# Attention and a routed mixture of experts on one core: splitting two of expert 0's weight chunks, wider products from expert 1 on, and a sum shared between ScalarE and VectorE

## The chip, the cores and the metric

The kernel runs on one NeuronCore of a Trainium2 chip. The metric is the device time of one execution in microseconds. Five engines with queues of their own work side by side: TensorE (PE, with its weight loads as PEld), VectorE (DVE), ScalarE (ACT), GpSimd (POOL) and SyncE (SP), which here only issues DMAs. TensorE writes its results to PSUM, of which the expert stage uses eight banks; all else lives in SBUF.

## What is computed

Causal attention over 4 batches of 12 heads, 448 rows of 64, feeds 1792 tokens of width 768 into a mixture of 8 experts. Tokens go to experts greedily by score, at most 224 to each; each expert applies two layers with a ReLU between.

```python
scores = np.where(mask, -1e9, scale * q @ k.T);  attn = softmax(scores)
x = (attn @ v).transpose(0, 2, 1, 3).reshape(1792, 768)
order = np.argsort(-(x @ w_gate).flatten())        # greedy, 224 tokens for each expert
for e in range(8):
    out[assigned == e] = np.maximum(x[assigned == e] @ w1[e], 0) @ w2[e]
```

## The kernel before

The program is written out by a planner. Each step is a task with an engine, an estimated duration, a priority and the tasks that it depends on; `Schedule.run` (line 117) gives each engine's next instruction to the ready task of highest priority, and fills TensorE's idle time with dummy products (`filler`, line 1130) until expert 0 starts. The order in each queue is thus fixed when the program is built, by estimated durations, and a queue that meets a wait holds everything behind it.

**Attention** runs over 24 pairs of heads: scores (line 218), masked exponential (228, 238), transposes of the probabilities (246), product with v (272), copy to `xt`. A pair's rows are then transposed back (`rows_at` and `rows_mm`, line 296), scaled by the reciprocal of the row sums into `xio` (320) and stored batch by batch to the DRAM buffer `xd` (325). Pairs from `LATE` = 10 on are not transposed there but in `late` (line 941), beside the routing of expert 0: four transposes of a pair into one PSUM bank of four that rotate, then each half of the bank (two of four blocks) scaled by ScalarE with four instructions (314) or by VectorE with two (320), whichever the planner finds free. `PIECES` says after which pairs a piece of a batch is stored.

**Routing** finds each expert's 224 tokens in turn by counting on TensorE (`rt`, lines 767, 784) and comparing on VectorE (666, 781, 750). `members` (813) turns the choice into indices: a one-hot `oh` of 128 positions (841) times token numbers (849), cast to `idx` (852). The steps of experts 0 and 1 have priority 10.9; from expert 2 on (`calm`, line 911) a VectorE step has 5.0 and a TensorE step is planned 0.4 us later. A gather by GpSimd (1121) brings an expert's rows from `xd`; for expert 0 it waits for all stores.

**Experts.** An expert's weights are eight chunks of 768 KB, four of the first layer and four of the second, fetched by SP (1100) into four raw buffers. Each chunk is split into `wh`, a rounded copy that ScalarE casts (1106), and `wl`, the remainder, three differences by VectorE (1112). Only the first four chunks of expert 0 (g < 4) are used whole. The inputs are split likewise (1160, 1165). A first-layer block f of 128 outputs is a sum over six d:

- expert 0: one float32 product of 224 columns each (1177), or two of 112 for f < 2;
- expert 1: three products of 224 columns (1184, 1185, 1186);
- from expert 2 on (`TWICE` = 2): one product of `wh` with both input parts side by side, 448 columns (1182), and one of `wl` with 224 (1186). The two halves of the bank are then added by a VectorE reduce (`mid_sum`, 1196).

ReLU and its split (1192, 1200) follow, then the second layer: three products for each of eight f, two halves of the rows and two of the columns (1212), eviction by ScalarE (1216) and scatter by GpSimd (1231). The tiles `ph`, three banks, take the first-layer sums in turn; the four `po` banks take the second layer's.

## Time and profile before

| | us |
|---|---|
| median of 3 runs | 503.19 (502.56 to 503.5) |
| the profiled execution | 503.2 |
| its span, first to last instruction | 501.5 |
| TensorE busy | 488.0 |
| VectorE busy | 394.5 |
| ScalarE busy | 292.9 |

The span is what the trace shows; 1.7 us of the execution's time lie outside it. A busy share is an average over stages with different limits, so the stages are read one by one. In a row of the timeline, the number in brackets is how long the engine sat idle before the instruction and what ended that.

### The profile page before, as it was taken

The numbers are of one execution on the slowest core, as the hardware profiler recorded it, in microseconds if no ns is written. First come the engines' busy times: TensorE is split into PE (matmuls) and PEld (weight loads), VectorE is DVE, ScalarE is ACT, GpSimd is POOL, SyncE is SP. The second block draws the span as 40 slices with busy tenths as digits, with TensorE's granted clock in tenths as the row PEclk, the third lists the DMA queues.
The fourth block names the chain that finished last, engine by engine and source line by source line (L and its number), as shares of the span: only waits on it lengthen the run. The fifth ranks groups of instructions, "written<-read, shape, count | busy, mean of one in ns | idle before, by whom it ended". The sixth has DMA issues, their size and how long they took to land.

```text
span 501.5 us, 10644 instructions
## 1 busy us (share of the span) xinstructions
PE 488.0 (97%) x3930; PEld 406.5 (81%) x3930; DVE 394.5 (79%) x1308; ACT 292.9 (58%) x741; POOL 51.8 (10%) x86
## 2 busy tenths in 40 slices
PE   8999999999999979999999999999999999999995
PEld 4666666666666665998999999999999999999995
DVE  4978777787789685688999999999999788687710
ACT  5988888989888571244545624444453545654410
POOL 5000000000000101010120120120211410110101
PEclk9999999999999999999999999999999999999999
DMA  8932182542000048766967663584672976858101
GB/s 230 302 109 99 38 269 63 184 148 75 2 2 1 1 121 253 257 195 191 320 217 247 220 213 127 160 289 139 219 234 79 349 242 225 286 181 308 57 1 55
DMA packets 19349, 84.08 MB, mean 168 GB/s; under 512 B 2272, under 2 KB 5280, under 8 KB 19296
## 3 DMA queue, kind: packets, MB, share of 16 engines
q1 hardware_dynamic: 16624, 72.36, 44.8%
q0 software_dynamic: 2672, 11.04, 7.1%
q8 instruction: 31, 0.51, 0.4%
q14 instruction: 22, 0.18, 0.1%
HBM read 72.38 MB, written 11.01 MB: 166 GB/s over the span
## 4 chain that ended last, share of the span: by engine, by line
PE 88%; DMA 4%; ACT 2%; POOL 2%; issue 1%; DVE 1%; POOLq 0%; DVEq 0%; ACTq 0%; SPq 0%
PE po L1212 26%; PE ph L1182 13%; PE t L246 10%; PE s L272 10%; PE ph L1186 7%; PE s L218 7%; PE t L218 2%; DMA xio<-xd,idx 2%; PE rt L767 2%; PE ph L1147 2%; PE t L296 1%; PE t L331 1%; PE po L1177 1%; PE ph L1184 1%; PE ph L1185 1%
## 5 line engine op out<-in xcount | busy, mean ns | idle before, releaser
L1112 DVE TENSOR_TENSOR wl<-wr,wh 128x512 fp32r<-128x512 f32 x180 | 115.9, 682 | 9.0 <-ACT wh L1106 9.0
L1106 ACT CAST wh<-wr 128x1536 fp32r<-128x1536 f32 x60 | 88.4, 1479 | 59.1 <-DMA wr<-in_w 58.9
L238 ACT ACTIVATE P<-Sm,mx 112x224 f32<-112x224 f32 (+2 forms) x192 | 99.1, 523 | 22.5 <-DVE mx L228 17.2
L1182 PE MATMUL ph<-xhl,wh 128*128 128x448 f32 x288 | 94.0, 380 | 0.0
L1186 PE MATMUL ph<-xhl,wl 128*128 128x224 f32 x336 | 89.7, 267 | 0.0
L1212 PE MATMUL po<-wh,HH 128*112 128x384 f32 x256 | 68.3, 343 | 0.0
L1212 PE MATMUL po<-wl,HH 128*112 128x384 f32 x256 | 68.0, 341 | 0.0
L1212 PE MATMUL po<-wh,HL 128*112 128x384 f32 x256 | 67.2, 338 | 0.0
L228 DVE CUSTOM_DVE_ANT_0 Sm<-s,MK 112x448 f32<-112x448 f32 (+1 forms) x144 | 59.6, 464 | 6.3 <-PE s L218 5.6
L1186 PEld LDWEIGHTS ph<-xhl,wl 128*128 128x128 f32 x336 | 64.2, 191 | 0.0
L1182 PEld LDWEIGHTS ph<-xhl,wh 128*128 128x128 f32 x288 | 54.2, 188 | 4.2
L246 PE MATMUL t<-idf,P 112*112 112x112 f32 x480 | 52.6, 262 | 0.4 <-ACT P L238 0.4
L272 PE MATMUL s<-PT,v 112*64 112x448 f32 (+3 forms) x384 | 50.6, 405 | 0.0
L246 PEld LDWEIGHTS t<-idf,P 112*112 112x112 f32 x480 | 45.8, 133 | 5.1 <-ACT P L238 1.5
L1192 ACT ACTIVATE HH<-hs 128x224 fp32r<-128x224 f32 x48 | 18.8, 391 | 49.0 <-DVE hs L1196 47.5
L1212 PEld LDWEIGHTS po<-wh,HL 128*112 128x112 f32 x256 | 43.9, 174 | 0.3
L1212 PEld LDWEIGHTS po<-wl,HH 128*112 128x112 f32 x256 | 43.3, 175 | 0.4
L252 ACT COPY PT<-t 112x448 f32<-112x448 f32 (+1 forms) x109 | 42.7, 465 | 1.2 <-PE t L246 1.1
L1212 PEld LDWEIGHTS po<-wh,HH 128*112 128x112 f32 x256 | 43.2, 175 | 0.2
L218 PE MATMUL s<-raw 64*112 64x112 f32 (+2 forms) x288 | 41.3, 414 | 0.1
L1196 DVE TENSOR_REDUCE hs<-ph 128x224 f32<-128x448 f32 x48 | 29.9, 622 | 14.3 <-PE ph L1186 10.0
L272 PEld LDWEIGHTS s<-PT,v 112*64 112x64 f32 x384 | 23.2, 136 | 21.3 <-issue 9.8
(169 smaller groups left out, 667.5 us busy)
## 6 DMA issues: line engine op xcount, KB each, us to landing
wr<-in_w SPq DMA_DIRECT2D x64, 768.0 KB, 5.0
raw<-in_qk SPq DMA_DIRECT2D x11, 896.0 KB, 8.0
v<-in_v SPq DMA_DIRECT2D x12, 448.0 KB, 3.7
xd<-xio SPq DMA_DIRECT2D x3, 672.0 KB, 4.0
xd<-xio SPq DMA_DIRECT2D x1, 1344.0 KB
xd<-xio SPq DMA_DIRECT2D x1, 896.0 KB, 5.4
xd<-xio SPq DMA_DIRECT2D x2, 448.0 KB, 3.7
raw<-in_qk SPq DMA_DIRECT2D x1, 448.0 KB
```

The costliest lines, as they stand in the source:

```text
L218: self.nc.tensor.matmul(ts[sd][:, o:o + m], q[:, 0, i * C:i * C + C], q[:, 1, :m], start=True, stop=True)
L228: self.nc.vector.tensor_tensor_reduce(Sm[:, QO[i]:QO[i] + m], self.S.pop((pp, sd, i)), self.MK[:, S - m:], -0.125, 3.0e38, OP.add, OP.min, ...
L238: self.nc.scalar.activation(P[:, s], Sm[:, s], AF.Exp, bias=mx[:, i:i + 1], scale=-1.0, accum_out=self.RS[b][:, pr, sd * NC + i:sd * NC + ...
L246: self.nc.tensor.transpose(t[:, o + (i - j) * C:o + (i - j) * C + C], P[:, QO[i] + j * C:QO[i] + j * C + C], self.k["idf"][:C, :C])
L252: self.nc.scalar.copy(out, x)
L272: self.nc.tensor.matmul(self.AV[pp][sd * 64:sd * 64 + 64, j * C:S], self.V[2 * pp + sd][:, j, :], self.PT[pp, sd][:, KO[j]:KO[j] + m], sta ...
L1106: self.nc.scalar.copy(hi, self.R[p, c])
L1112: self.nc.vector.tensor_sub(lo[:, s], self.R[p, c][:, s], hi[:, s].bitcast(F32))
L1182: nc.tensor.matmul(t[:, :2 * CAP], hi[:, s], x[:, d].rearrange("p z t -> p (z t)"), start=d == 0, stop=False)
L1186: nc.tensor.matmul(t[:, :CAP], lo[:, s], x[:, d, 0], start=False, stop=d == 5)
L1196: self.nc.vector.tensor_reduce(t, self.P[p, f][:, :2 * CAP].rearrange("p (z t) -> p t z", z=2), axis=AX.X, op=OP.add)
L1212: self.nc.tensor.matmul(self.T[p, "o", u][z][:, :384], a[p][:, f, u * C:u * C + C], w[:, o:o + 384], start=f == 0 and n == 0, stop=f == 7 ...
```

## The change

- `PLAIN` = 2: expert 0's first two chunks stay whole; its third and fourth are split as all others are, and f = 4 to 7 of expert 0 use the products of 448 and 224 columns. Expert 0's inputs are split for this after they have been copied whole (`turn_hi`, `turn_lo` on `X[0, 0]`).
- `TWICE` = 1: expert 1 uses these products too.
- Where they are used, ScalarE first copies the second half of the sum to SBUF (`mid_copy`), and VectorE adds it to the first half in place of the reduce.
- `LATE` = 12: pairs 10 and 11 have their rows transposed within attention. The late pairs' halves get a PSUM tile each, in a ring of six: the four `po` banks and two of `ph`. VectorE scales a half with one instruction.
- The one-hot has 112 positions and not 128, in one buffer kept for all experts.
- The routing steps of expert 1 are `calm` too.

```diff
-LATE = 10
-PIECES = {11: 2, 14: 3, 17: 3, 20: 3, 22: 2, 23: 1}
+LATE = 12
+PIECES = {14: 3, 17: 3, 20: 3, 22: 2, 23: 1}
-TWICE = 2
+TWICE = 1
+PLAIN = 2
     def rows_dve(self, pp, t, blocks=range(NC)):
-        for s in (slice(0, NC),) if len(blocks) == NC else (slice(i, i + 1) for i in blocks):
-            self.nc.vector.tensor_tensor(...)
+        s = slice(blocks[0], blocks[-1] + 1)
+        self.nc.vector.tensor_tensor(...)
-    k["io"] = cs.tile([C, 128, 2], F16, name="io")
+    k["io"] = cs.tile([C, C, 2], F16, name="io")
-            shape = [C, s.stop - s.start, 128, 2]
+            shape = [C, s.stop - s.start, C, 2]
-        calm = self.p > 1
+        calm = self.p > 0
     def late(self):
+        spare = [self.ps.tile([C, 512], F32, name="ph", bufs=3) for _ in range(2)]
+            for h in range(2):
+                m, box = 2 * n + h, {}
+                def mm(i, pp=pp, m=m, box=box):
+                    if i % 2 == 0:
+                        box["t"] = self.bank(m % 6) if m % 6 < 4 else spare[m % 6 - 4]
+                    at.rows_mm(pp, box["t"], (i,))
+                a = act.get(m - 6, [])
...
     def weights(self, p, cs):
-                deps += self.use[g - 4] if g < 8 else self.lo[g - 4]
+                deps += self.use[g - 4] if g - 4 < PLAIN else self.lo[g - 4]
-            if g < 4:
+            if g < PLAIN:
                 self.lo[g] = [self.got[g]] * 3
                 continue
     def expert(self, p):
+                    if u:
+                        h = add("ACT", 0.43, lambda d=d: self.turn_hi(0, d, (0, 1)), ts[d], 7.5)
+                        xs.append(add("DVE", 0.54, lambda d=d: self.turn_lo(0, d, (0, 1)), [h], 7.5))
+            half, plain = p == 0 and f < SPLIT, p == 0 and f < 2 * PLAIN
+            twice = p >= TWICE or p == 0 and not plain
-            if p >= TWICE:
-                deps = [add("DVE", 0.55, lambda p=p, f=f: self.mid_sum(p, f), deps + (hl[-2:-1] if f else []), 8.0)]
+            if twice:
+                c = add("ACT", 0.3, lambda p=p, f=f: self.mid_copy(p, f), deps, 8.5)
+                deps = [add("DVE", 0.31, lambda p=p, f=f: self.mid_sum(p, f), [c] + (hl[-2:-1] if f else []), 8.0)]
     def first(self, p, f, d, u=None):
-        if p == 0:
+        if p == 0 and f < 2 * PLAIN:
...
-        if p >= TWICE:
+        if p >= TWICE or p == 0:
+    def mid_copy(self, p, f):
+        t = self.Hc[p, f] = self.sb.tile([128, CAP], F32, name="hc", bufs=2)
+        self.nc.scalar.copy(t, self.P[p, f][:, CAP:2 * CAP])
     def mid_sum(self, p, f):
-        self.nc.vector.tensor_reduce(t, self.P[p, f][:, :2 * CAP].rearrange("p (z t) -> p t z", z=2), axis=AX.X, op=OP.add)
+        self.nc.vector.tensor_tensor(t, self.P[p, f][:, :CAP], self.Hc.pop((p, f)), op=OP.add)
```

## Rows read from the trace of the kernel before

**Rows 1.** Page, part 1: busy time, share of the span and instructions of each engine.
```profile
PE 488.0 (97%) x3930; PEld 406.5 (81%) x3930; DVE 394.5 (79%) x1308; ACT 292.9 (58%) x741; POOL 51.8 (10%) x86
```
**Rows 2.** Waits of TensorE, whole span: us in total, times, longest us.
```profile
PE rt L784 <- DVE cd L781: 2.0, 3, 1.2
PE ph L1147 <- DMA xio<-xd,idx: 1.4, 2, 0.9
...
PE rt L779 <- DVE cd L776: 0.6, 1, 0.6
```
**Rows 3.** Busy time by stages: stretch, us, busy us of each engine (instructions), clock, DMA.
```profile
0.00:175.00 175.00, 172.83 (x1400) 114.14 (x1401) 133.48 (x558) 145.66 (x502) 8.76 (x30) 1.00 0.36 109
...
201.00:208.00 7.00, 6.95 (x87) 6.89 (x87) 4.18 (x16) 1.95 (x7) 0.00 (x0) 1.00 0.86 321
208.00:216.00 8.00, 7.46 (x83) 6.66 (x82) 5.12 (x23) 2.45 (x4) 0.00 (x0) 1.00 0.45 131
216.00:225.40 9.40, 9.31 (x65) 9.11 (x65) 8.89 (x38) 3.90 (x5) 1.97 (x3) 1.00 0.75 239
225.40:231.00 5.60, 4.93 (x45) 3.92 (x44) 4.85 (x13) 1.84 (x2) 0.00 (x0) 1.00 0.98 291
231.00:247.00 16.00, 16.00 (x149) 14.57 (x148) 14.50 (x43) 7.94 (x9) 0.00 (x0) 1.00 0.68 231
247.00:265.80 18.80, 18.80 (x205) 18.66 (x204) 18.11 (x57) 10.83 (x16) 5.67 (x6) 1.00 0.73 236
265.80:303.90 38.10, 38.10 (x344) 35.11 (x343) 36.25 (x106) 19.11 (x24) 5.00 (x6) 1.00 0.65 209
```
**Rows 4.** Chain that ended last, expert 0's unsplit products: start, us, what.
```profile
218.29 1.99 PE ph L1177 x10
```
**Rows 5.** Timeline of TensorE in expert 2's first layer: start, us, instruction.
```profile
292.20 0.37 PE L1182 MATMUL ph<-xhl,wh 128*128 128x448 f32 x1
292.41 0.27 PE L1186 MATMUL ph<-xhl,wl 128*128 128x224 f32 x1
292.51 0.37 PE L1182 MATMUL ph<-xhl,wh 128*128 128x448 f32 x1
```
**Rows 6.** Timeline of TensorE in expert 1's first layer.
```profile
248.74 0.28 PE L1184 MATMUL ph<-xhl,wh 128*128 128x224 f32 x1
...
249.07 0.27 PE L1184 MATMUL ph<-xhl,wh 128*128 128x224 f32 x1
```
**Rows 7.** Groups of instructions by form: count, busy us, mean ns of one, idle before.
```profile
L1112 DVE TENSOR_TENSOR wl<-wr,wh 128x512 fp32r<-128x512 f32 x180 | 115.9, 682 | 9.0 <-ACT wh L1106 9.0
L1106 ACT CAST wh<-wr 128x1536 fp32r<-128x1536 f32 x60 | 88.4, 1479 | 59.1 <-DMA wr<-in_w 58.9 <-DVE wl L1112 0.2
L1196 DVE TENSOR_REDUCE hs<-ph 128x224 f32<-128x448 f32 x48 | 29.9, 622 | 14.3 <-PE ph L1186 10.0 <-issue 3.0 <-PE rt L784 0.8
L1165 DVE TENSOR_TENSOR xhl<-ph,xhl 128x448 fp32r<-128x448 f32 x21 | 11.8, 618 | 2.7 <-ACT xhl L1160 2.6
L1200 DVE SCALAR_TENSOR_TENSOR HL<-ph,HH 128x224 fp32r<-128x224 f32 x14 | 5.4, 384 | 0.3 <-ACT HH L1192 0.3
L1154 ACT COPY xhl<-ph 128x224 f32<-128x224 f32 x6 | 1.9, 350 | 12.9 <-PE ph L1147 12.9
```
**Rows 8.** DMA issues from 200.2 to 200.6 us: KB, median us to landing.
```profile
wr<-in_w SPq DMA_DIRECT2D x1, 768.0 KB, 8.1
```
**Rows 9.** Chain that ended last, row transposes of one pair in attention.
```profile
62.46 0.63 PE t L296 x4
```
**Rows 10.** Chain that ended last, from 190 to 232 us.
```profile
190.97 4.11 DMA xd<-xio
...
196.08 4.14 DMA xio<-xd,idx
...
222.46 8.08 DMA xio<-xd,idx
```
**Rows 11.** Timeline of VectorE, attention's end and the late stretch.
```profile
173.01 0.39 DVE L254 COPY xt<-s 128x224 f32<-128x224 f32 x1 [1.40 <-ACT xt L252]
...
184.10 0.88 DVE L320 TENSOR_TENSOR xio<-po,rs 112x128 f32<-112x128 f32 x4 [0.92 <-ACT xio L314]
...
194.82 0.16 DVE L852 CAST idx<-rt 112x2 int32<-112x2 f32 x1 [0.40 <-PE rt L849]
```
**Rows 12.** Busy time of VectorE's weight differences (line 1112) by stretches.
```profile
200.00:225.00 25.00, 2.03 (x3) 1.00 0.69 228
225.00:230.00 5.00, 2.57 (x4) 1.00 0.95 280
```

More of the change, by code (lines that the diff above doesn't have):

```diff
@@ L1028, in expert @@
         f1, hh, hl = [], [], []
-        long = 0.4 if p == 0 else 0.314 if p >= TWICE else 0.338
         if p == 0:
@@ L1036, in expert @@
             g = 8 * p + f // 2
-            half = p == 0 and f < SPLIT
+            half, plain = p == 0 and f < SPLIT, p == 0 and f < 2 * PLAIN
+            twice = p >= TWICE or p == 0 and not plain
+            long = 0.4 if plain else 0.314 if twice else 0.338
             for d in range(6):
-                deps = ts[d // 2] + [self.lo[g][d // 2], f1[-1] if f1 else None]
+                deps = (xs[d // 2:d // 2 + 1] if p == 0 and not plain else ts[d // 2]) + [self.lo[g][d // 2], f1[-1] if f1 else None]
                 if d == 0 and not half:
@@ L1053, in expert @@
             if not half:
-                self.ph.append(free if p >= TWICE else [hl[-1]])
+                self.ph.append(free if twice else [hl[-1]])
         self.f1 = [f1[-1]]
@@ L1133, in filler @@
         if (0, 0) in self.T and not self.moved:
-            if any(t.end is None for t in self.lact[NP - LATE - 1]):
+            if any(t.end is None for t in self.lact[max(self.lact)]):
                 return
@@ L1159, in turn_hi @@
         t = slice(us[0] * C, us[-1] * C + C)
[L1160 removed]
+        x = self.T[p, d] if p else self.X[0, 0][:, 2 * d:2 * d + 2, 0]
+        self.nc.scalar.copy(self.X[p][:, 2 * d:2 * d + 2, 0, t], x[:, :, t])
     def turn_lo(self, p, d, us):
```

52 lines of the change are left out of this document (26 added, 26 removed).

## The prediction

> **What bounds the kernel now.** I began with the totals: TensorE is busy 488.0 us of the 501.5 us span, VectorE 394.5, ScalarE 292.9 [rows 1]. A share of busy time proves little, so next came the list of what TensorE waits for [rows 2]: over the whole span its named waits add up to a few microseconds, all of them before 231 us. From there on it never waits, and the time of a stage is the sum of what TensorE has to issue. Third, the busy time by stages [rows 3]: attention ends near 174.8 us, the stretch from 175 to 201 us holds the late rows and expert 0's routing, expert 0's first products run from 201 to 225.4 us and its second products to 247 us, expert 1's first products from 247 to 265.8 us. In expert 1 TensorE is busy without a gap, while VectorE is busy 18.11 of 18.80 us beside it: it is the second bound, one step behind. So an edit pays where it shortens TensorE's stream or the stretch before 201 us, and VectorE decides whether the gain is kept.
>
> **Expert 0's split chunks.** A product of the unsplit kind is two instructions of 224 columns; ten instructions take 1.99 us [rows 4], so a product takes 0.400 us. A split product with the 448-column form is one instruction of 448 and one of 224 columns: from 292.20 to 292.51 us, 0.315 us [rows 5]. Chunks 3 and 4 hold f = 4 to 7 with six products each: 24 x (0.400 - 0.315) = 2.04 us less on TensorE, directly on the path.
>
> **Expert 1's 448-column products.** Its three 224-column products start at 248.74 and the next three at 249.07 us [rows 6]: 0.333 us against 0.315 us, 48 times, 0.86 us less. [...]
>
> **What the split adds.** Two ScalarE casts of 1.479 us, six VectorE differences of 0.682 us, three ScalarE casts and three VectorE differences of expert 0's inputs (0.618 us each) [rows 7]. ScalarE is busy only 1.95 of 7 us from 201 us and 2.45 of the next 8 us [rows 3], which hides its share. Is the split in time? Chunk 3 was asked for in the window at 200.2 to 200.6 us and landed 8.1 us later, by 208.7 us at the latest [rows 8]; cast and three differences end near 212.5 us, and f = 4 comes on TensorE behind 24 half products and 12 full ones, about 213 to 214 us. Chunk 4 follows some two microseconds behind and is wanted two microseconds later. So by a hair yes, as long as VectorE is free for it. The buffers of these two chunks are now released by their differences and not by their last product, which lets the next two fetches on SP's queue start earlier, not later.
>
> **The sum by halves.** The reduce over 448 elements took 0.622 us on VectorE; the new form is a ScalarE copy of 224 elements (nearest row: the copy of the same size from PSUM, 0.350 us) and an add on VectorE, whose nearest row is the two-input operation on 128x224 from the same bank, 0.384 us [rows 7]. VectorE saves 0.24 us on each of 48, but pays 0.38 us on 12 new ones (four of expert 0, eight of expert 1). No TensorE time hangs on either while the bank comes back in time: three banks rotate, a group takes 6 x 0.315 = 1.9 us, and copy plus add plus two hand-overs take about 0.9 us, with a queued cast of 1.48 us ahead of the copy 2.4 us, against 3.8 us allowed. I put it at nothing; if that cover is gone, a wait is at most one cast, 1.5 us.
>
> **Two pairs more inside attention.** LATE = 12 moves pairs 10 and 11 into attention, where TensorE has no slack: four row transposes took 0.63 us there [rows 9], so 2 x 0.63 = 1.26 us more. VectorE (133.5 of 175 us [rows 3]) hides the two scalings. Their piece of the store goes out as part of one larger store long before it is needed, and SP's queue then holds one issue less in the late stretch.
>
> **Late rows and expert 0's routing.** Two chains end together: the last store issued at 190.97 us lands 4.11 us later [rows 10], and the indices are ready at 194.82 + 0.16 = 194.98 us [rows 11]. Both must shorten. The late chain loses 4 of its 28 halves; it took from 174.8 to 190.9 us, so 4/28 of 16.1 us is 2.3 us. The routing chain runs through VectorE, and there late halves stand in front of it while they wait: the one at 184.10 us sat 0.92 us until a scaling of ScalarE had ended, and the routing's next step waited behind it. I read this as the two halves of one bank; that readers of one bank are put one after the other is seen cleanly at 173.01 us: VectorE's copy of the other half of a bank sat 1.40 us and started when ScalarE's copy ended [rows 11]. [...] With each half in a bank of its own these waits lose their cause. TensorE's waits for the routing's cd in this stretch, 2.0 us [rows 2], are the nearest row for what is lost; the smaller one-hot adds 0.2 us. The bounds are 0 (routing waits for something else) and 3.6 us (every late half out of its way); I take 2.2 us, the smaller of the two chains' gains.
>
> **Calmer routing of expert 1.** Its VectorE steps lose their rank over the expert's work, and its TensorE steps are planned later. It removes the wait of 0.6 us that TensorE has behind the routing's last round [rows 2]. The indices of expert 1 come some microseconds later; its rows landed at 230.5 us (222.46 + 8.08 [rows 10]) and are needed only at 247 us. The wait of 0.5 us for that gather may shrink or grow by as much; I leave it.
>
> **The new load on VectorE.** From 201 to 265.8 us VectorE was busy 4.18 + 5.12 + 8.89 + 4.85 + 14.50 + 18.11 = 55.65 us of 64.8 [rows 3]: 9.1 us free. Added are 6 x 0.6 for the differences as they follow each other, 3 x 0.55, and 12 x 0.33: 9.2 us, in a stretch that is to become 2.9 us shorter. So VectorE is full, and some 3 us of it, routing of expert 2 and later weights, slides behind 265.8 us. There, experts 2 to 4 give back 8 x 0.24 = 1.9 us each. What stands in the queue behind is the differences of the second layer's weights: seven were done by 230 us (three before 225 and four after [rows 12]), just ahead of TensorE. If routing steps go in front, TensorE waits for them. Before the second products 6.6 us of the additions must fit (3.6 for the differences, 1.65 for the inputs, 1.3 for expert 0's four sums), 2.9 us earlier than now. Free there are 5.7 us before 216 us [rows 3], just where chunks 3 and 4 arrive, and the routing of experts 1 and 2 gives way by being planned later. I put the wait at 0.6 us, between 0 and 6 us.
>
> **The sum**, against the profiled execution (span 501.5 us, its time 503.2 us, 1.7 us outside; the median of the three runs is 503.19): -2.04 - 0.86 - 0.6 + 1.26 - 2.2 + 0.6 = -3.8 us. Forecast: 499.4 us.
>
> **Rivals.** (1) The start doesn't move: routing is limited by its own steps, the halves cost it nothing, and the 1.26 us of attention are paid for nothing. For it: the routing's steps wait for one another, late halves or not; against it: the 0.92 us that one late half alone stood in front of it. Then -3.84 + 2.2 = -1.64: 501.6 us, up to 502.2. (2) VectorE takes TensorE's place between 213 and 247 us: the lowest-ranked differences of chunks 3 to 7 come behind the routing. Priced: 6.6 us of added work plus 2.9 us of earlier need is 9.5 us, less the 5.7 us free 3.8 us; where the free time is only half hit, 6.6 us. It turns the sign from a wait of 4.4 us on; with 6 us the time is 504.8 us. Against it: experts 2 and 3 run with VectorE 95% busy (36.25 of 38.10 us [rows 3]) and TensorE waits for nothing there. (3) In between, a wait of 3 to 5 us eats the gain: 502.2 to 504.2 us. [...] (5) The new form doesn't save VectorE time, because add and reduce cost alike: then experts 2 to 4 stay as full as now, which cost TensorE nothing; 499.4 us stands, or rival 2 follows.
>
> **How the numbers follow.** Forecast case with its own spread of 497 to 500.8 us: 0.53. Rival 1: 0.19. Rival 3: 0.10. Rival 2: 0.14. Rival 4: 0.04. A measurement of this kernel can tell about 0.2%, 1.0 us, from no change. Faster by more than that: the forecast, rivals 1 and 4, 0.76; within: rival 3, 0.10; slower: rival 2, 0.14. The range runs from all terms at their good ends (-2.04 - 0.86 - 0.6 + 1.26 - 3.6 and the gather's 0.5, -6.3: 496.8 us) to within rival 3, 503.4 us, which leaves out rival 2 and little below.
>
> **What the new profile would show.** Expert 0's f = 4 to 7 as pairs of 448 and 224 columns each 0.315 us apart; expert 1 likewise; attention 1.26 us longer; the first transposes of expert 0 some 21.5 to 24.5 us behind attention's end, against 25.4 now; no VectorE idle for ScalarE at the late scalings. Wrong would be: TensorE waits with wl or xhl as the cause between 210 and 250 us (rival 2), a gap between attention and expert 0 as long as before (rival 1), or a late gather in front of expert 1.

## The result and the profile after

The changed kernel took 510.9 us (median of 4 runs, 508.52 to 511.69) beside 503.35 us of the kernel before (502.56 to 505.19) on the same chip: a ratio of 1.0149 [1.0118, 1.018], slower by 7.5 us where 3.8 us less was forecast. The profiled execution took 510.58 us with a span of 508.9 us, 7.4 us more than the span before.

The totals first, as in [rows 1]: TensorE's busy time hardly moved, VectorE's fell by 4.3 us and ScalarE's grew by 20.5 us. They don't show where 7 us went.

```profile
PE 489.0 (96%) x3885; PEld 405.7 (80%) x3885; DVE 390.2 (77%) x1313; ACT 313.4 (62%) x803; POOL 50.6 (10%) x87
```

What TensorE waits for, whole span (us in total, times, longest), as in [rows 2]:

```profile
PE ph L1161 <- DMA xio<-xd,idx: 6.8, 5, 3.2
PE rt L787 <- DVE cd L784: 2.5, 2, 2.3
PE t L177 <- DVE zero L174: 1.3, 1, 1.3
PE ph L1161 <- DVE hs L1216: 1.2, 1, 1.2
```

The transposes (line 1161) wait 6.8 us for gathered rows, 1.4 us before. Two other waits are new: 2.3 us in one piece near 209 us for the routing's `cd`, where the longest before was 1.2 us, and 1.2 us of a transpose for a sum. (`cd` and `G` are results of the routing's comparisons on VectorE, lines 784 and 669 of the changed kernel.)

Busy time by stretches (columns as in [rows 3]; clock and DMA share are the third and second from the end): the granted clock falls from 1.00 to 0.50 at 417.3 us, 1.9 us behind the end of the first of two long waits for rows, and stays there for 6.83 us (0.73 and 0.58 are means of stretches).

```profile
376.00:410.00 34.00, 32.80 (x243) 30.83 (x242) 29.66 (x82) 19.02 (x29) 8.79 (x8) 1.00 0.68 220
410.00:415.00 5.00, 2.25 (x15) 1.87 (x13) 3.49 (x8) 3.91 (x6) 0.16 (x2) 1.00 0.97 270
415.00:420.00 5.00, 3.35 (x19) 3.09 (x20) 0.64 (x2) 1.21 (x3) 0.00 (x0) 0.73 0.39 137
420.00:425.00 5.00, 5.00 (x19) 4.77 (x18) 5.00 (x9) 2.93 (x3) 0.00 (x0) 0.58 0.46 135
```

The same in the starts of TensorE's stages, us from the span's start:

| stage | before | after | after - before |
|---|---|---|---|
| first transposes of expert 0 | 200.26 | 196.10 | -4.2 |
| second products of expert 1 | 265.5 | 261.5 | -4.0 |
| second products of expert 4 | 379.5 | 376.0 | -3.5 |
| transposes of expert 6 reached | 412.2 | 412.2 | 0 |
| second products of expert 5 | 412.5 | 415.8 | +3.3 |
| second products of expert 6 | 445.7 | 453.1 | +7.4 |
| last product | 495.3 | 502.7 | +7.4 |

Up to 376 us the change is 3.5 to 4 us ahead, as much as the forecast wanted. By 412.2 us the lead is gone: 1.2 us for the wait for a sum at 378 us, and some 2 us for transposes of expert 5 and routing of experts 6 and 7 that the kernel before had done ahead of 379.5 us. That part of the lead was only borrowed. The other 7.4 us are lost between 412 and 425 us, in a stage in which nothing of the change was expected to matter. The chain that ended last shows the place (start, us, what):

```profile
393.78 4.92 POOL idh L1241 x2
...
398.89 0.99 POOL out L1251
...
400.19 6.87 DMA out<-xio,idx
...
409.13 8.95 DMA xio<-xd,idx
418.08 0.04 issue
418.12 1.38 PE ph L1161 x6
```

Expert 4's output rows are scattered at 398.9 and 400.2 us; they leave a buffer, `xio`, into which expert 6's rows are then gathered, so the gather waits for the scatter's landing (6.87 us) and its own second half lands 8.95 us after its issue. TensorE's order has the transposes of expert 6 in front of the second products of expert 5, and TensorE stands there from 412.2 us on. The rows that write or read `xio` in the kernel before, from 395 to 420 us, and in the changed one, from 405 to 421 us, show the same dependence with another landing time (the last line gives minimum, median and maximum of the indirect transfers in view; before, that is two scatters and the gather's second half):

```profile
L1121 POOL DMA_INDIRECT xio<-xd,idx x2: 946/949/952, 406.6 to 407.8; - x2
...
  POOL xio L1121: 7.2, 1
...
DMA to landing us min/median/max: 4.6/6.8/7.3
```

```profile
L1135 POOL DMA_INDIRECT xio<-xd,idx x2: 942/946/951, 407.9 to 409.1; - x2
...
DMA to landing us min/median/max: 7.4/8.2/8.9
```

Before, the second half was issued at 407.82 and landed 4.6 us later, at 412.4 us, 0.9 us ahead of the first transpose that reads it. Of the first half, issued at 406.57, the last of the 16 semaphore updates of its landing stands in the trace at 411.5 us, 0.6 us ahead of the first transpose at 412.16 us. GpSimd waited 7.2 us for its buffer there too, and nothing on TensorE's list of waits said so. After, the first half was issued 1.3 us later and took 7.4 us, till 415.3 us, the second half till 418.1 us. So TensorE came at the same time, and the rows came 3.8 and 5.7 us later. The 16 DMA engines were busy 0.94 of the time from 396.9 to 412.2 us, 0.82 before; that is beside it, not shown to be its cause.

### The profile page after: what moved, and what is told of

It is laid out like the page before. It is cut to its first block, busy times and chain, and to the rows that moved or that the text cites. A ratio compares the mean times of both kernels' runs of the same rounds, so it can differ in the third digit from the quotient of the medians.

```text
span 508.9 us, 10618 instructions
## 1 busy us (share of the span) xinstructions
PE 489.0 (96%) x3885; PEld 405.7 (80%) x3885; DVE 390.2 (77%) x1313; ACT 313.4 (62%) x803; POOL 50.6 (10%) x87
## 4 chain that ended last, share of the span: by engine, by line
PE 70%; DVE 13%; DMA 9%; issue 3%; POOL 2%; ACT 2%; POOLq 0%; SPq 0%; ACTq 0%; DVEq 0%
PE po L1232 17%; PE ph L1198 10%; PE t L247 10%; PE s L273 10%; PE s L219 7%; PE ph L1202 5%; DVE wl L1126 5%; DMA wr<-in_w 4%; DMA xio<-xd,idx 4%; PE t L219 2%; DVE G L669 2%; PE t L297 1%; PE ph L1161 1%; DMA out<-xio,idx 1%; PE rt L770 1%
## 5 line engine op out<-in xcount | busy, mean ns | idle before, releaser
L1126 DVE TENSOR_TENSOR wl<-wr,wh 128x512 fp32r<-128x512 f32 x186 | 119.9, 683 | 9.9 <-ACT wh L1120 9.9
L1120 ACT CAST wh<-wr 128x1536 fp32r<-128x1536 f32 x62 | 91.6, 1483 | 57.8 <-DMA wr<-in_w 44.8
L1198 PE MATMUL ph<-xhl,wh 128*128 128x448 f32 x360 | 118.5, 382 | 0.0
L1202 PE MATMUL ph<-xhl,wl 128*128 128x224 f32 x360 | 95.6, 266 | 0.0
L1198 PEld LDWEIGHTS ph<-xhl,wh 128*128 128x128 f32 x360 | 67.8, 188 | 5.5 <-issue 0.2
L1232 PE MATMUL po<-wh,HL 128*112 128x384 f32 x256 | 69.1, 346 | 0.0
L1202 PEld LDWEIGHTS ph<-xhl,wl 128*128 128x128 f32 x360 | 68.9, 191 | 0.0
L219 PEld LDWEIGHTS s<-raw 64*112 64x112 f32 x288 | 26.8, 173 | 14.7 <-issue 5.5
L1208 ACT ACTIVATE HH<-hs 128x224 fp32r<-128x224 f32 x60 | 23.4, 392 | 23.4 <-DVE hs L1216 23.4
```

Of the source, the lines that this page charges most:

```text
L219: self.nc.tensor.matmul(ts[sd][:, o:o + m], q[:, 0, i * C:i * C + C], q[:, 1, :m], start=True, stop=True)
L1120: self.nc.scalar.copy(hi, self.R[p, c])
L1126: self.nc.vector.tensor_sub(lo[:, s], self.R[p, c][:, s], hi[:, s].bitcast(F32))
L1198: nc.tensor.matmul(t[:, :2 * CAP], hi[:, s], x[:, d].rearrange("p z t -> p (z t)"), start=d == 0, stop=False)
L1202: nc.tensor.matmul(t[:, :CAP], lo[:, s], x[:, d, 0], start=False, stop=d == 5)
L1208: self.nc.scalar.activation(self.HH[p][:, f], self.P[p, f][:, :CAP], AF.Relu)
```

## The experiments

All ratios are against the kernel before on the same chip, with a 95% interval. "Waits" is the sum of what the list of TensorE's waits shows from 175 to 495 us, "clock" half of the time in which the granted clock was at its lower level, 0.50, from 170 to 492 us, both of the profiled execution; "rest" is its span less both, the time in which TensorE worked at full clock and what lies at the ends. (In the changed kernel two second-layer products take 0.64 us at 421 us, at the lower level, and 0.34 us at 425 us, at 1.00. Half is an upper bound: of the 6.83 us at 417.3 us the first 0.8 us are themselves wait, of those in idh_later 2.4 us.)

| kernel | median us | ratio | span | waits | clock | rest |
|---|---|---|---|---|---|---|
| before | 503.35 | 1 | 501.5 | 5.4 | 1.7 | 494.4 |
| after | 510.9 | 1.0149 [1.0118, 1.018] | 508.9 | 11.6 | 5.1 | 492.2 |
| turn6_later | 506.98 | 1.0072 [1.0039, 1.0105] | 504.8 | 9.9 | 1.7 | 493.2 |
| idh_later | 509.42 | 1.010 [1.007, 1.0131] | 508.4 | 11.8 | 3.4 | 493.2 |
| fetch6_held | 510.32 | 1.011 [1.0036, 1.0184] | 510.9 | 13.9 | 3.4 | 493.6 |
| calm_from_2 | 505.89 | 1.0062 [1.0032, 1.0093] | 502.1 | 8.1 | 1.7 | 492.3 |
| transposes_later | 500.04 | 0.9933 [0.9903, 0.9964] | 498.8 | 5.0 | 1.7 | 492.1 |
| late_rows_alone | 498.96 | 0.992 [0.9896, 0.9945] | 498.8 | 2.8 | 0 | 496.0 |
| weights_alone | 511.42 | 1.0199 [1.0141, 1.0256] | 506.6 | 11.8 | 1.7 | 493.1 |
| reduce_kept | 508.27 | 1.012 [1.0052, 1.0187] | 506.3 | 10.4 | 1.7 | 494.2 |
| own_row_tiles | 503.45 | 1.0008 [0.9986, 1.0029] | 500.7 | 7.6 | 0 | 493.1 |
| casts_later | 500.56 | 0.9944 [0.9924, 0.9964] | 498.5 | 4.2 | 1.7 | 492.6 |
| pair_form_alone | 505.56 | 1.0036 [1.0, 1.0072] | 504.5 | 7.4 | 1.7 | 495.4 |
| tiles_and_casts | 503.06 | 0.998 [0.9959, 1.0002] | 502.4 | 6.1 | 3.4 | 492.9 |
| no_differences | 500.62 | 0.995 [0.9929, 0.997] | 499.1 | 5.2 | 0 | 493.9 |
| one_chunk_split | 501.82 | 0.997 [0.9941, 0.9999] | 503.0 | 5.8 | 3.4 | 493.8 |
| pair_form_later | 503.31 | 1.0014 [0.9992, 1.0037] | 502.8 | 4.5 | 1.7 | 496.6 |
| before_later | 503.54 | 1.0006 [0.9984, 1.0028] | 502.2 | 5.8 | 1.7 | 494.7 |
| own_halves_10 | 501.19 | 0.997 [0.9944, 0.9996] | 501.4 | 6.4 | 0 | 495.0 |
| pairs_12_shared | 502.86 | 1.0013 [0.9984, 1.0043] | 504.1 | 5.9 | 1.7 | 496.5 |

The last column is the main reading. The nine kernels that hold the whole change but for an order or a buffer (after, turn6_later, idh_later, fetch6_held, calm_from_2, transposes_later, own_row_tiles, casts_later, tiles_and_casts) have a rest of 492.1 to 493.6 us; late_rows_alone and pairs_12_shared, with the products of before and 12 pairs in attention, 496.0 and 496.5. By this the work became 2.4 to 4.4 us shorter, where 2.9 was counted. The column is no finer than some 1.5 us: weights_alone against before, both with 10 pairs, gives 1.3 us. What decides the time is the two columns before it.

### Which wait makes it slower

Theory A says that TensorE stands in its order behind expert 6's (and 7's) rows, and that half the clock follows. First, one number of the planner for one expert:

```diff
-            x.append(add("DMA", 0.96, lambda: None, [a], 9.0, (1.0, 2.0)[u] if p == 0 else 5.0))
+            x.append(add("DMA", 0.96, lambda: None, [a], 9.0, (1.0, 2.0)[u] if p == 0 else 10.0 if p == 6 else 5.0))
```

> The changed kernel with one edit: the gather of expert 6's rows is planned to take 10 us to land and not 5, so that TensorE's transposes of these rows stand some 14 pairs of products into expert 5's second layer and not in front of it. Theory A (the loss is TensorE waiting in order for a late gather, 3.4 and 1.5 us, and the halved clock behind it, some 3.4 us): no idle TensorE at 412 to 418 us, no halved clock there, 8 us less than the changed kernel, 502 to 504 us. Theory B (VectorE, fuller by the added splits and sums, starves TensorE of weights): the wait goes over to products of expert 5 or 6, 509 to 511 us. Theory C (the clock falls by itself): the clock still falls near 417 us.

Some 4 us came back. No halved clock is left from 265 to 492 us, but 4.0 us of waits for rows remain there in four pieces, the longest 1.2 us: two for expert 6 and two, at 448 and 450 us, for expert 7. The gather of expert 6 was still late, so its transposes merely waited less, and the next expert's waited too.

Two runs asked what made the gather late. GpSimd's index halves ahead of the scatter (line 1241, 4.92 us in the chain above) were put behind the scatters:

```diff
-            half = add("POOL", 0.2, lambda p=p: self.halves(p), [self.ix[p]], 4.0)
+            half = add("POOL", 0.2, lambda p=p: self.halves(p), [self.ix[p]] + self.scat[p - 1], 4.0)
```

> The changed kernel with one edit: GpSimd's two instructions that make the last expert's half indices (4.92 us together) stand behind expert 6's scatter and not in front of expert 4's. Theory A1 (they hold back expert 4's scatter and with it expert 6's gather, and the gather's own 9 us is the rest): scatter 1.5 to 2 us earlier, gather lands near 416 us and not 418, 2 to 4 us less, 507 to 509 us. Theory A2 (they are the whole cause): the gather lands before TensorE wants it at 412 us, 502 to 504 us. Theory B (VectorE starves TensorE): 510 to 511 us.

The first scatter left 3.3 us and the gather 1.4 us earlier (395.6 and 406.5 us), but the gather's halves then took 9.0 and 9.2 us, TensorE waited 4.8 us and the clock was halved for 6.8 us from 413.2 us. GpSimd's order by itself doesn't explain the lateness. Then the fetches of expert 6's weights were planned behind its gather:

```diff
+            if p == 6:
+                deps += self.landed
             self.got[g] = add("DMA", 2.185, lambda p=p, c=c: self.fetch(p, c), deps, 4.0 - 0.01 * g, 0.95 if p == 0 else 2.5, 1.1)
...
+        if p == 6:
+            self.landed = x[1:]
+            self.weights(p, range(8))
```

> The changed kernel with one edit: the fetches of expert 6's weights wait until its rows have been gathered, so that fewer weight transfers share the DMA engines with that gather. Theory A3 (the gather is slow because a burst of weight fetches runs beside it, DMA share 0.94 to 0.99): it lands within 5 us of its issue, near 413 to 414 us, the waits shrink from 4.9 to some 2 us, 503 to 507 us, unless the weights of expert 6, now later, make TensorE wait at its first layer. Theory A1 (GpSimd's order): gather issued at the same 407.9 and 409.1 us, lands late all the same, 510 us. Theory B: 511 us or more.

This run is inconclusive. It orders the issues but makes no queue wait; the fetches still went out beside the gather, waits of 4.3 and 3.4 us stand at 415 and 453 us, and nothing was learnt of crowding. Whether a gather lands late because weight fetches run beside it stays open.

The full test of theory A, for all experts:

```diff
+            x.append(add("DMA", 0.96, lambda: None, [a], 9.0, (1.0, 2.0)[u] if p == 0 else (7.0 if p == 1 else 14.0)))
```

> The changed kernel with one planner number altered: the landing time that the order assumes for the gathered rows of experts 1 to 7 is 7 us (expert 1) and 14 us (the others) where it was 5, so that the transposes of the next expert stand further back in TensorE's order. Theory A (the loss is TensorE standing in its order behind the late rows of experts 6 and 7, and the halved clock that follows): no wait of over 1 us for a gather after 300 us, no stretch with the clock at half after 400 us, the second products of expert 6 start before 450 us, time 499 to 502 us. Rival (the transfers as a whole are late and some other wait, for weights, takes the place): the wait comes back for wl or the fetches, 505 us or more.

Theory A holds: 500.04 us, 11 us less than the change, faster than before. The instructions are the same as in the change; what differs is their order. What TensorE waits for in it, from 265 us on, is one line:

```profile
PE rt L787 <- DVE cd L784: 0.3, 1, 0.3
```

Is it a cure of this harm or a gain that the kernel before could have had as well? The same edit in the kernel before:

> The kernel before with the same later landing assumed for the gathered rows (7 and 14 us), and nothing else of the change. It had no wait for gathered rows behind 231 us, so by theory A nothing is gained: within 0.2% of before. If the order itself is worth time apart from late rows, it is faster by 1 us or more, and the gain of transposes_later is in part not a cure of the change's harm.

The time is 503.54 us, no change (1.0006 [0.9984, 1.0028]): planning for later rows was worth nothing while the rows came in time.

The other way to cure it takes away what the gather waits for. Gathered rows go to one persistent tile, output rows to another, in the same memory; what waits for the scatter of two experts back is now the eviction and not the gather:

```diff
-            deps = [self.ix[p], touch] if p < 2 else [self.ix[p]] + self.scat[p - 2]
+            deps = [self.ix[p], touch] if p < 2 else [self.ix[p]] + self.turned[p - 2]
...
-                a = [add("ACT", 0.41, lambda p=p, u=u, z=z: self.evict(p, u, z), [prev], 9.0) for z in zs]
+                a = [add("ACT", 0.41, lambda p=p, u=u, z=z: self.evict(p, u, z), [prev] + self.scat.get(p - 2, []), 9.0) for z in zs]
...
-        self.nc.gpsimd.indirect_dma_start(out=self.IO[p][:, u], out_offset=None, in_=self.xd,
+        self.nc.gpsimd.indirect_dma_start(out=self.IO[0][:, 2 * (p % 2) + u], out_offset=None, in_=self.xd,
...
-        self.nc.scalar.copy(self.IO[p][:, 2 + u, z * 384:z * 384 + 384], self.T[p, "o", u][z][:, :384])
+        self.nc.scalar.copy(self.IO[1][:, 2 * (p % 2) + u, z * 384:z * 384 + 384], self.T[p, "o", u][z][:, :384])
...
```

> The changed kernel with one dependence removed: gathered rows lie in one persistent tile and output rows in another, two experts' places in each, so that the gather of expert p no longer waits until the scatter of expert p-2 has landed. The planner's numbers stay. Theory A (the late gather of expert 6 begins with that dependence: it was issued at 407.9 us, 14 us behind its indices): it is issued within 3 us of its indices, no wait for gathered rows above 1.2 us after 300 us, no halved clock after 400 us, 498.5 to 502 us. Rival (the gather is late because transfers crowd: its landing takes 8 us or more wherever it is issued and TensorE still stands before it): 505 us or more.

The dependence is confirmed: expert 6's gather leaves at 387.7 us, 0.4 us behind its indices (20.2 us behind them in the changed kernel, not the 14 of the expectation), and no late row and no halved clock is left from 300 to 492 us. The rows of `xio` from 384 to 420 us:

```profile
L1136 POOL DMA_INDIRECT xio<-xd,idx x4: 933/952/3544, 387.7 to 397.5; - x4
...
DMA to landing us min/median/max: 5.4/8.7/11.4
```

The landing is as slow as ever, up to 11.4 us, and nobody waits for it. The time, 503.45 us, missed the expected 498.5 to 502 us: 6.0 us of waits stay behind 200 us, the largest 1.5 us for the routing's `cd` and 1.5 us for expert 1's rows.

### Which part of the change brings it

First the weight part was taken out:

```diff
-TWICE = 1
+TWICE = 2
-PLAIN = 2
+PLAIN = 4
-        calm = self.p > 0
+        calm = self.p > 1
...
-                c = add("ACT", 0.3, lambda p=p, f=f: self.mid_copy(p, f), deps, 8.5)
-                deps = [add("DVE", 0.31, lambda p=p, f=f: self.mid_sum(p, f), [c] + (hl[-2:-1] if f else []), 8.0)]
+                deps = [add("DVE", 0.55, lambda p=p, f=f: self.mid_sum(p, f), deps + (hl[-2:-1] if f else []), 8.0)]
```

> The changed kernel without its weight part: expert 0's chunks 3 and 4 are not split, 448-column products start at expert 2, the sum of two halves is one reduce, the routing of expert 1 keeps its rank. What is left of the change: 12 pairs in attention, the late halves in six tiles, the smaller one-hot. Theory A (the start gained some 4 us by itself; the loss comes of the weights' part, which shifts the routing and the release of the raw buffers): expert 0's transposes start near 196 us and the time is 499 to 500.5 us. Rival (a start 4 us earlier by itself makes later transfers collide): gathers of experts 5 to 7 that take 7 us or more, 503 us or more.

The time is 498.96 us, as theory A wanted, and the lowest of all: 4.4 us less than before with half of the change. Its waits from 200 us on:

```profile
PE ph L1160 <- DMA xio<-xd,idx: 0.7, 2, 0.5
PE rt L787 <- DVE cd L784: 0.3, 1, 0.3
PE ph L1160 <- DVE hs L1215: 0.3, 1, 0.3
```

It too starts earlier than before, by 3.2 us, and reaches expert 6's transposes at 409.4 us; but here scatter (394.3 us) and gather (402.1 us, landed 6.2 us later) moved forward with it. So being early is not enough to make rows late: in the changed kernel they didn't move with TensorE. The other half, with the late part undone:

```diff
-LATE = 12
-PIECES = {14: 3, 17: 3, 20: 3, 22: 2, 23: 1}
+LATE = 10
+PIECES = {11: 2, 14: 3, 17: 3, 20: 3, 22: 2, 23: 1}
...
-                        box["t"] = self.bank(m % 6) if m % 6 < 4 else spare[m % 6 - 4]
+                    box["t"] = self.bank(n % 4)
```

> The changed kernel with its late part undone: 10 pairs in attention, two halves of a late pair share a PSUM tile, everything about the weights as changed. Theory A: expert 0's transposes start near 200 us as before, the products of experts 0 and 1 are shorter by some 2.9 us, and the wait for expert 6's rows with its halved clock comes all the same: 505 to 513 us. Rival (the collision needs the earlier start too): no late gather, 500 to 502 us.

At 511.42 us the weight part, with the calmer routing in it, does the harm with and without the earlier start. By which wait is shown less well here: its profiled execution, 508.33 us and so below its median, has 2.7 us of waits for rows at 416 and 451 us and no halved clock behind them; another 5.1 us of waits lie between 200 and 265 us.

Of the weight part, the form of the sum alone was then put back:

> The changed kernel with the sum of the two halves as one reduce on VectorE, as before the change, in place of the ScalarE copy and the add; all else as changed. Theory A (order and late rows decide, not the sum's form): the time stays at 506 to 513 us, and VectorE is busy some 0.24 us more on each of 60 sums. Rival C (the copies queue behind ScalarE's casts, which delays the sums, the turn of expert 5 at 378 us and VectorE's later differences): the wait at 378 us is gone and the time falls to 504 us or less. Rival D (VectorE's relief is worth something): 513 us or more, with new waits of TensorE for VectorE between 205 and 265 us.

With the reduce in place of copy and add (the last three lines of the diff of late_rows_alone, and the reduce in `mid_sum`) the time is 508.27 us: the form of the sum doesn't carry the loss. Neither rival came true as put: a shorter wait for a sum (0.3 us) is left at the transposes of expert 5, beside a wait of 1.7 us for `HL`, and waits of 1.7 and 1.8 us for routing are there between 205 and 260 us.

### Where the weight part's 2.9 us went

transposes_later has no late rows, and its products are shorter by 2.9 us than those of late_rows_alone; yet both take about the same. In the profile of transposes_later the list of waits from 200 to 265 us and two stretches of the busy time show the price:

```profile
PE rt L787 <- DVE cd L784: 2.8, 1, 2.8
```

```profile
205.00:210.00 5.00, 2.19 (x26) 1.94 (x25) 2.44 (x7) 4.20 (x6) 0.00 (x0) 1.00 0.48 167
210.00:215.00 5.00, 5.00 (x34) 4.48 (x33) 3.84 (x12) 1.59 (x3) 0.00 (x0) 0.66 0.58 174
```

TensorE waits, and VectorE is busy only 2.44 of those 5 us: it isn't full, it waits itself. The chain in the changed kernel, where the same wait, 2.3 us, ends at 208.84 us, tells for what:

```profile
196.10 8.61 DMA wr<-in_w
...
205.04 1.47 ACT wh L1120
206.51 0.26 ACT HH L1208
206.78 0.02 issue
206.80 0.58 DVE HL L1220 x2
207.39 0.02 issue
207.41 1.28 DVE wl L1126 x2
208.69 0.10 DVE cd L784 x2
208.79 0.04 issue
208.84 0.16 PE rt L787
```

Chunk 3's fetch takes 8.61 us. Its new cast (line 1120) stands on ScalarE's queue ahead of the activations of products long done; they wait behind it, VectorE's `HL` (line 1220) waits for them, the routing's `cd` stands behind `HL`, and TensorE's next routing step (line 787) stands ahead of its products. ScalarE stood idle for 3.2 us ahead of that cast. Theory E was that chain; rival F, that VectorE is simply full. In transposes_later's order the casts were then moved behind three activations:

```diff
-            self.got[g] = add("DMA", 2.185, lambda p=p, c=c: self.fetch(p, c), deps, 4.0 - 0.01 * g, 0.95 if p == 0 else 2.5, 1.1)
+            self.got[g] = add("DMA", 2.185, lambda p=p, c=c: self.fetch(p, c), deps, 4.0 - 0.01 * g, (0.95 if c < PLAIN else 6.0) if p == 0 else 2.5, 1.1)
```

> The kernel of transposes_later with one more planner number altered: the landing assumed for expert 0's weight chunks 3 and 4 (and its later ones) is 6 us in place of 0.95, so that ScalarE's casts of them stand behind the activations of the first three products in its order. In transposes_later TensorE stood 3.16 us at 209.6 us and had half its clock for the next 3.41 us, which costs 3.16 + 1.7 = 4.9 us. Theory E (a cast that waits for its transfer holds the activation behind it, that holds VectorE, that holds the routing step for which TensorE waits): the wait is gone and the time is 500.0 - 4.9 = 495.2 us, 494.5 to 497. Rival F (VectorE is simply full there, as the prediction's second rival has it): the wait moves on to a later step, 498.5 to 501 us.

Theory E was right on the place and wrong on the time. The wait at 209 us is gone and the second products of expert 0 start at 218.2 us where transposes_later had 222.9. But the time is 500.56 us: at 229 us a new wait stands, 1.9 us for the routing's `G` on VectorE, with 3.41 us of halved clock behind it. To see whether VectorE's added work makes that one, the six differences of chunks 3 and 4 were left out:

```diff
-                          for z in range(3)]
+                          for z in range(3)] if g > 3 else [self.hi[g]] * 3
...
-        self.W[p, c] = (hi, lo)
+        self.W[p, c] = (hi, lo if p or c > 3 else hi)
```

> The kernel of casts_later with the six VectorE differences of expert 0's chunks 3 and 4 left out, some 3.6 us of VectorE before 230 us; the products take the cast part twice in their place, so that TensorE's instructions are as many and as long, and the result lacks the low part of these weights. casts_later lost 2.2 us at 229.3 us to routing on VectorE and 1.7 us to the halved clock behind. If VectorE's fullness is the cause: no TensorE wait above 0.8 us between 200 and 240 us, no halved clock there, 500.6 - 3.9 = 496.7 us (495.5 to 498). If it is the order of the queues: the wait stays in its place or moves by a step, 499 to 501 us.

It doesn't. With 3.6 us less on VectorE the time is 500.62 us and the wait stays in its place, ending at 230.1 us. TensorE's waits from 200 to 265 us:

```profile
PE rt L770 <- DVE G L669: 2.4, 1, 2.4
```

VectorE is busy 6.05 of 10 us from 210 to 220 us here and 9.59 of the next 10: what it has to do in the second stretch comes to it late. That speaks for the order and against the amount. Further runs fit this:

```diff
-PLAIN = 2
+PLAIN = 3
```

> The kernel of transposes_later with only chunk 4 of expert 0 split, chunk 3 left as before: the products give 1.02 + 0.86 us in place of 2.9, and VectorE has half the added differences, with none of ScalarE's casts before chunk 4's. If VectorE's fullness takes the gain: the wait near 209 us is below 1 us and no halved clock follows; 498.96 - 1.9 = 497.1 to 498.5 us. If the added work isn't the cause (the routing of expert 1 gives way, whatever is split): a wait of 2 to 3 us stays, 500 us or more.

With half the added work (on top of transposes_later) there is still 1.9 us of wait in one piece near 210 us with half the clock behind it, and a second such pair, 1.4 us of wait, at 283 us for an `xhl` difference. The time is 501.82 us; less work on VectorE didn't make it faster. In the changed kernel itself the routing's rank was put back:

```diff
-        calm = self.p > 0
+        calm = self.p > 1
```

> The changed kernel with one edit undone: routing steps of expert 1 keep their high rank, as before the change. Theory D (the calmer routing of expert 1 puts every later expert's indices 6 to 13 us later, and the last one's hold GpSimd's queue in front of expert 4's scatter): indices of expert 7 near 387 us, the scatter of expert 4 near 397 us, the late gather gone, 501 to 505 us, though TensorE waits some more for splits at 213 to 230 us. Theory B (VectorE's load): the same 509 to 511 us or worse, since the routing now stands in front of the splits.

Expert 1's routing with its old rank keeps the rows of expert 6 in time (gather at 405.1 us, its halves landed 4.8 and 6.3 us after their issues), 505.89 us. By the ratios more than half of the change's loss goes with it; in exchange TensorE waits 2.0 us for `cd` near 207 us and 4.1 us for `G` till 225 us, with half the clock from 226.1 us. The rank moves a part of the loss and doesn't remove it.

Next came the 448-column form in expert 1 alone, on late_rows_alone, and the same with later transposes (`TWICE = 1` in place of 2, and the planner's line of transposes_later):

> The kernel of late_rows_alone with expert 1's products in the 448-column form, their sums by the reduce: 48 products of three 224-column instructions become pairs. By the rows (0.333 against 0.315 us) 0.86 us less than late_rows_alone's 499.0: 498.1 us, 497.5 to 498.7. [...] Rival (eight reduces of 0.62 us more on a VectorE that is 95% busy beside expert 1): waits of TensorE for VectorE between 245 and 300 us, 499.5 us or more.

> The kernel of pair_form_alone (late rows, 448-column products from expert 1 on, reduce, no split of chunks 3 and 4) with the gathered rows planned to land 7 us (expert 1) and 14 us (others) after their issue, as in transposes_later. Theory A (pair_form_alone lost its time only to the late rows of expert 6 and the halved clock): 498.96 - 0.86 = 498.1 us, 497.3 to 498.9, no wait above 1 us behind 300 us. Rival (the form itself costs time beside a full VectorE): 499.5 us or more.

They took 505.56 and 503.31 us, where 498.1 was wanted of both: theory A failed here in its numbers. The first lost 4.5 us to late rows of expert 6, with half the clock from 414.3 us, and so shows that this collision needs neither split nor copies. The second has no late rows; it waits 1.5 us for `G`, 0.7 for `wl` and 0.7 for `cd` between 200 and 495 us, with 3.4 us of halved clock from 262.5 us, and its rest of 496.6 us is 1.5 us above what the form should give, which stays unexplained. So the gain of the form in expert 1 doesn't show in these two times. Last, both cures together:

> The changed kernel with both cures: separate tiles for gathered and output rows as in own_row_tiles, and a landing of 4.5 us assumed for expert 0's chunks 3 and 4 and later ones, so that their casts stand further back on ScalarE. Theories A and E together: no wait over 1.5 us on TensorE behind 200 us, 494.5 to 497.5 us, faster than before and than late_rows_alone. If E is wrong (VectorE is full there): 498.5 to 501 us.

The time is 503.06 us, with waits for `G` of 2.8 us in three pieces and 6.8 us of halved clock from 228 us. No version with the split weights was faster than late_rows_alone.

### What the start was worth

The forecast gave the start 0.9 us (2.2 less 1.26); late_rows_alone gained 4.4. Two kernels, both edits of late_rows_alone, take it apart:

```diff
-LATE = 12
-PIECES = {14: 3, 17: 3, 20: 3, 22: 2, 23: 1}
+LATE = 10
+PIECES = {11: 2, 14: 3, 17: 3, 20: 3, 22: 2, 23: 1}
```

> The kernel of late_rows_alone with the two pairs taken out of attention again (10 pairs in attention, 14 late, the store in pieces as before); the late halves keep their six PSUM tiles. If the tiles bring the gain (no half waits for the other engine's half, TensorE's 2.0 us of waits for the routing's cd between 175 and 201 us and the halved clock behind them are gone): expert 0's transposes start near 197 us or earlier, 498.5 to 500.5 us. If the moved pairs bring it: TensorE waits about 2 us in that stretch as before, the start is near 200 us, 502 us or more.

```diff
-        s = slice(blocks[0], blocks[-1] + 1)
-        self.nc.vector.tensor_tensor(...)
+        for s in (slice(0, NC),) if len(blocks) == NC else (slice(i, i + 1) for i in blocks):
+            self.nc.vector.tensor_tensor(...)
...
-                        box["t"] = self.bank(m % 6) if m % 6 < 4 else spare[m % 6 - 4]
+                    box["t"] = self.bank(n % 4)
```

> The kernel of late_rows_alone with the late halves again two to a PSUM tile, as before the change; 12 pairs stay in attention. If the tiles bring the gain: attention is 1.3 to 1.7 us longer, the late stretch shorter by the 2.3 us of four halves at most, the waits for the routing's cd stay: start near 199 us, 502 to 503.5 us. If the moved pairs bring it: start near 197 us, 498.5 to 500.5 us.

The moved pairs don't bring it. With own tiles and only 10 pairs in attention expert 0's transposes start at 196.5 us; with 12 pairs and shared tiles at 201.4 us, no faster than before. Busy time from 185 to 190 us and TensorE's waits from 174 to 201 us, first pairs_12_shared, then own_halves_10:

```profile
185.00:190.00 5.00, 3.60 (x48) 2.83 (x48) 3.61 (x21) 3.99 (x20) 0.00 (x0) 0.83 0.50 155
...
PE rt L787 <- DVE cd L784: 2.0, 3, 1.2
```

```profile
185.00:190.00 5.00, 4.82 (x55) 3.20 (x53) 3.95 (x19) 2.15 (x11) 0.09 (x1) 1.00 0.96 295
...
PE rt L787 <- DVE cd L784: 0.2, 1, 0.2
```

Shared tiles go with 2.0 us of waits and 3.41 us at half clock, from 188.3 us; own tiles with neither. But pairs_12_shared takes back a second thing, VectorE's one instruction for a half. VectorE's scalings from 175 to 197 us in pairs_12_shared (with its wait for ScalarE's half), then in own_halves_10:

```profile
L321 DVE TENSOR_TENSOR xio<-po,rs x22: 273/280/292, 179.2 to 190.0; 112x128 f32<-112x128 f32 x22
...
  ACT xio L315: 1.7, 3
```

```profile
L321 DVE TENSOR_TENSOR xio<-po,rs x10: 411/416/420, 176.3 to 185.4; 112x256 f32<-112x256 f32 x10
```

A half takes VectorE 0.56 us in two instructions and 0.42 us in one, 1.6 us for eleven halves, beside the 1.7 us of waits. No run has one without the other, so tiles and single instruction together bring the earlier start; how it divides between them is not shown. The median of own_halves_10 is 501.19 us, on a chip where the kernel before took 502.73; 3 us of waits for routing steps stand from 213 us on in its order. So the start is worth about 4 us by the stage, and what arrives at the end is again decided by the later waits.

## Why the prediction was wrong

**The failed step** is in the first paragraph of the prediction, "From there on it never waits, and the time of a stage is the sum of what TensorE has to issue." It read a list with no waits behind 231 us [rows 2] as if there were room. There was less than 1 us: the gather of expert 6 hangs on the scatter of expert 4 by a shared buffer, and its two halves came 0.6 and 0.9 us ahead of TensorE. The prediction followed gathers up to expert 1 and took every microsecond gained before 265.8 us as one gained at the end. In the changed kernel expert 6's rows came 3.8 and 5.7 us later than before, to a TensorE that came no earlier, and cost 3.2 and 1.2 us of waits and about 3.0 us for the 6.05 of 6.83 us at half clock that were no wait: 7.4 us, its whole loss. transposes_later and own_row_tiles show it, each by another edit that ends these waits; before_later shows that the first of them is worth nothing without them. Why a gather in this stretch took 4.2 us in one kernel and 9 us in another stays open.

**The products** held by their spacing. In the changed kernel's timeline of TensorE the pairs of expert 1 stand 0.31 to 0.32 us apart, as [rows 5] had it:

```profile
245.64 0.38 PE L1198 MATMUL ph<-xhl,wh 128*128 128x448 f32 x1
245.86 0.27 PE L1202 MATMUL ph<-xhl,wl 128*128 128x224 f32 x1
245.96 0.38 PE L1198 MATMUL ph<-xhl,wh 128*128 128x448 f32 x1
```

The sum of the work terms, -2.04 - 0.86 + 1.26 = -1.64 us, would take the rest in the table from 494.4 to 492.8 us; after has 492.2. The pairs of expert 0 stand as close, at 215.08, 215.39 and 215.70 us. The 0.86 us of expert 1 are no more than what pair_form_alone and pair_form_later left unexplained.

**The sum by halves** cost what its nearest rows said (0.384 and 0.350 us in [rows 7]):

```profile
L1216 DVE TENSOR_TENSOR hs<-ph,hc 128x224 f32<-128x224 f32 x60 | 23.2, 388 | 16.6 <-ACT hc L1212 16.2
L1212 ACT COPY hc<-ph 128x224 f32<-128x224 f32 x60 | 20.6, 343 | 22.1 <-PE ph L1202 21.1 <-PE rt L782 0.5
```

Its wait was put at nothing and, without cover, "at most one cast, 1.5 us": once, at 378 us, a transpose waited 1.2 us for such a sum.

**The late stretch** was mis-sized: with attention the forecast had 0.9 us, and expert 0's first transposes came 4.2 us earlier. They stand 20.7 us behind the first late transpose, against 25.4 before, where 21.5 to 24.5 were forecast; and that first late transpose came 0.5 us later than before, where 1.26 us of attention were counted. The mechanism was right: VectorE's 1.7 us of waits for ScalarE's half, there before and in pairs_12_shared, are gone in the changed kernel and in own_halves_10, whose halves have tiles of their own. What the sum missed is a number beside the one it read: the clock from 185 to 190 us in the kernel before. Waits of 2.0 us were counted, the 3.41 us at half clock behind them (up to 1.7 us more) were not, and neither was VectorE's shorter scaling of a half.

```profile
185.00:190.00 5.00, 4.70 (x47) 3.88 (x47) 4.47 (x23) 4.92 (x24) 0.00 (x0) 0.66 0.63 202
```

**The calmer routing** removed the 0.6 us, but expert 1's gather left at 230.1 us in place of 221.2, and the wait for its rows grew to 1.8 us. The text had said that the wait of 0.5 us might "shrink or grow by as much". It had the rows wanted only at 247 us, but the transposes that read them stood at 229.3 us already, and the two halves now landed 8.8 and 9.6 us after their issues.

**The new load on VectorE**, rival 2, was put at 0.6 us between 0 and 6. It cost 2.3 us of wait and 1.7 us of clock near 209 us, inside the bounds, by another mechanism: a cast that waits for its transfer blocks a queue. The 1.7 us is again an upper bound. The prediction had compared busy times ("ScalarE is busy only 1.95 of 7 us ... which hides its share") and the arrival of chunk 3, by 208.7 us at the latest, with its own use at 213 us. The delay was in what is queued behind the cast, not in the chunk. casts_later shows it: with the casts behind three activations that wait is gone. What makes the later waits for `G` isn't settled: no run separated a smaller VectorE load from a changed order completely, since every edit moves the whole order; no_differences and one_chunk_split speak for the order.

**Rival 4**, a smaller gain from expert 1's products, was the author's estimate, and no run shows its term: the rows above have a pair in 0.31 to 0.32 us, where three products took 0.333 us before [rows 6]. The times of pair_form_alone and pair_form_later don't decide it.

## What to carry to other kernels

A bound engine that waits for nothing is not one with slack (expert 6's rows came 0.6 and 0.9 us ahead of TensorE): before counting a gain at its start, go through each later transfer that it needs, find what releases it, and compare when it lands with when the engine arrives. In the changed kernel a cast that waited for a fetch of 8.61 us left ScalarE idle for 3.2 us and held what was queued behind it, and TensorE waited 2.3 us; so an added cast is costed by its transfer's landing and by the neighbours in its queue, not by its busy time. When a change gives less than its counted work, split the span into waits, time at lower clock and the rest: here the rest fell by 2.2 us, where 1.6 was counted, and the other two rose by 9.6 us.

## What the runs showed of the hardware

Most of TensorE's waits of about 2 us or more that are told above had 3.41 or 6.83 us of granted clock at the lower level, 0.50, with them, but not all: one of 2.4 us in no_differences, one of 2.0 us near 207 us in calm_from_2 and one of 2.1 us near 209 us in fetch6_held had none. The lower level began between 2.4 us ahead of a wait's end (idh_later) and 1.9 us behind it (the changed kernel), and it came with shorter waits too, as the 1.4 us in one_chunk_split. So the price of such a wait, with half of that time counted, is estimated at its own length to 3.4 us more. Gathers of 112 rows each, for experts 6 and 7, landed between 4.2 us (transposes_later) and 11.4 us (own_row_tiles) after their issue, in one stage of kernels that differ in little.
